# Loading the first channel weight of a mixer as full rows, in two halves of the contraction

## The chip, the cores and the metric

The kernel runs on one core of a Trainium2 chip. The metric is device time in microseconds (us) of one execution. The runs of one kernel are compared by their median; the profile is of one execution.

## What is computed

The input is a batch of 8, with 8 heads, 576 positions and a head size of 64. Attention is masked to a sliding window (heads 0 to 3: the last 32 positions; heads 4 to 7: every fourth of the last 128). Its output, 576 x 512 for each batch element, goes through a mixer over tokens and then one over channels:

```
x  = attention(q, k, v)                    # [8, 576, 512]
h  = relu(x^T @ w_tok1) @ w_tok2           # over the 576 tokens, 256 hidden
u  = x + h^T
h2 = relu(u @ w_ch1) @ w_ch2               # over the 512 channels, 1536 hidden
out = u + h2
```

The change concerns `w_ch1`, a 512 x 1536 matrix of float32 in memory, which the kernel holds as float16 on the chip for all eight batch elements.

## The kernel before

All matrix work is in float16 with float32 sums. Of the batch elements one (`b`) is in its channel mixer on TensorE, while the next ones are in their scores, their values and their token mixer. The order is written by hand: `gen_main(b)` yields the channel mixer piece by piece, and `interleave` puts the other steps between its pieces, by due times that are constants in the last loop of the kernel. Each engine works through its own list in that order and waits at an instruction whose input is not there; what stands behind it on the same engine waits too.

The channel mixer of one batch element is twelve blocks of 128 hidden channels (`mb`). For each block, TensorE sums four matmuls into a bank `gp`, one for each 128 of the 512 channels (`cb`), with a 128 x 128 piece of `w_ch1` as the weights. `w3_block(cb, mb)` names that piece. For batch element 0 the order of `cb` is 0, 1, 2, 3. Then twelve more matmuls for each output block sum into `yp`, with `w_ch2`. In rows of the profile and in rows of the order, the tiles of all weights are called `w`, so that `w_0`, `w_1` and `w_2` stand for `w3_0`, `w3_1` and `w3_2`.

`w3` is three tiles of 128 x 4 x 512. Tile `i` holds the columns 512 i to 512 i + 511 of all four `cb`, and so the blocks `mb` = 4 i to 4 i + 3. `load_w3(i)` loads one; the transfer reads 512 runs of 512 float32 and writes them as float16 (512 KB written). It is issued from GpSimd's queue (POOL), since it changes the type; the loads of q, k and v go through SyncE's queue (SP). Both queues are served by the same 16 DMA engines.

What surrounds the loads on POOL, in the start-up of the kernel: `cast_vd(0, 0)` and `cast_vd(0, 2)` cast the two halves of v of the dilated heads of batch element 0 to float16, from `l_vd`; `cast_vx` casts the last piece, from `l_vx`, for which TensorE waits in `values`. Then two copies make `w2p`, and `gate` writes one element of the tile `lt` of batch element 1. The first load of batch element 1 on SP overwrites that tile, so that all loads of batch element 1 start after it. The casts of batch element 1 (`casts1`: tails `c_t`, then q and k by turns into `c_q` and `c_k`) follow on POOL, and TensorE transposes their results (`tp_q`, `tp_k`, line 309).

Of the kernel before, what the change touches and what calls it, by code (L numbers as in the profile page):

```python
# [22 lines left out]
DCH = 1536  # L23
# [45 lines left out]
def kernel(  # L69
# [11 lines left out]
    nc = tc.nc  # L81
# [4 lines left out]
    def fixed(name, shape, dtype=FP16):  # L86
        return sb.tile(shape, dtype, tag=name, bufs=1, name=name)
# [3 lines left out]
    def bank(tag, bufs, name, dtype=FP32):  # L91

        if tag in turn:
            turn[tag] += 1
            tag, bufs = f"{tag}{turn[tag] % bufs}", 1
        return ps.tile([128, 512 if dtype == FP32 else 1024], dtype, tag=tag, bufs=bufs, name=name)

    def copy(eng, out, in_):
        if eng is nc.scalar:
            nc.scalar.copy(out=out, in_=in_)  # L100
        else:
            eng.tensor_copy(out=out, in_=in_)  # L102

    def relu(eng, out, in_):
        if eng is nc.scalar:
            nc.scalar.activation(out=out, in_=in_, func=AF.Relu)  # L106
        else:
            eng.tensor_scalar_max(out=out, in0=in_, scalar1=0.0)  # L108
# [39 lines left out]
    w2a = fixed("w2", [128, 2, 640])  # L148
    w2 = [w2a[:, i] for i in range(2)]
    w2p = [fixed(f"w2p_{i}", [128, 4, 128]) for i in range(2)]  # L150
    w3 = [fixed(f"w3_{i}", [128, 4, 512]) for i in range(3)]
    w4a = fixed("w4", [128, NMB, DM])
    w4 = [w4a[:, i] for i in range(NMB)]
    idle = fixed("idle", [128, 512])
# [109 lines left out]
    def cast_vn(b, s, eng):  # L264
        copy(eng, vv[b % 2][:, s, 0:4, 0:64], l32[(b, "vn")][:, s])

    def cast_vd(b, h, eng):
        copy(eng, vv[b % 2][:, 0:4, 4 + h:6 + h, 0:64],
             l32[(b, "vd")][:, h:h + 2].rearrange("m h r d -> m r h d"))
# [22 lines left out]
    def u16(b, s):  # L292
        if b not in u16w:
            u16w[b] = sb.tile([128, 4, 4, 128], FP16, tag="u16", bufs=2, name=f"u16_{b}")
        return u16w[b][:, :, s]

    def blocks4(ap):
        return ap.rearrange("p (x c) -> p x c", c=128)
# [448 lines left out]
    def gen_main(b):  # L747
        odd = b % 2
        order = CBS if b else range(4)
        m0 = 640 * odd  # L750

        def w3_block(cb, mb):
            return w3[mb // 4][:, cb, mb % 4:512:4]

        def gp_tails(g):
            p = bank("main", 3, f"gt_{b}_{g}")
            for i in range(4):
                for cb in order:
                    nc.tensor.matmul(  # L759
                        out=p[:, 128 * i:128 * i + 128], lhsT=w3_block(cb, 4 * g + i), rhs=uT[(b, cb)][1],  # L760
                        start=(cb == order[0]), stop=(cb == order[-1]))
            relu(nc.scalar, gta[:, 4 * g:4 * g + 4, 512:640],
                 p.rearrange("p (i t) -> p i t", t=128))

        for mb in range(NMB):
            p = bank("main", 3, f"gp_{b}_{mb}")
            for i, cb in enumerate(order):
                nc.tensor.matmul(out=p, lhsT=w3_block(cb, mb), rhs=uT[(b, cb)][0], start=(i == 0), stop=(i == 3))  # L768
                if i == 1:
                    yield 0.43  # L770
            relu(nc.vector if (mb % 2 == 1 if b == 0 else mb % 4 != 3 if b == 1 else mb in (1, 5)) else nc.scalar, gta[:, mb, m0:m0 + 512], p)
            yield 0.43
            if odd and mb in (3, 6, 9):
                gp_tails(mb // 3 - 1)
                yield 0.9
        last = b == B - 1
        for s in ((4, 0, 1, 2, 3) if odd else (0, 1, 2, 3)):
            p = bank("main", 3, f"yp_{b}_{s}")
            o32 = sb.tile([128, DM], FP32, tag="o32", bufs=4, name=f"o32_{b}_{s}")
            if s < 4:  # L780
                for half in range(2):
                    c = slice(256 * half, 256 * half + 256)
                    if last and s == 3 and half:
                        p = bank("main", 3, f"yq_{b}_{s}")
                    for mb in range(NMB):
                        a0 = m0 + (s if half else 128 * s)
                        nc.tensor.matmul(  # L787
                            out=p[:, c],
                            lhsT=gta[:, mb, a0:m0 + 512:4] if half else
                            gta[:, mb, a0:a0 + 128],  # L790
                            rhs=w4[mb][:, c], start=(mb == 0), stop=(mb == NMB - 1))
                        if mb == 5:
                            yield 0.65
                    if last and s == 3:
                        nc.vector.tensor_tensor(out=blocks4(o32[:, c]), in0=blocks4(p[:, c]), in1=u16(b, s)[:, 2 * half:2 * half + 2], op=ALU.add)
                    elif half:
                        nc.vector.tensor_tensor(out=blocks4(o32), in0=blocks4(p), in1=u16(b, s), op=ALU.add)  # L797
                    if half or (last and s == 3):
                        for i in ((half,) if last and s == 3 else (0, 1)):
                            d = slice(256 * i, 256 * i + 256)  # L800
                            o = out[b, 0:512, d].rearrange("(m r) c -> r m c", r=4)[s] if i else \
                                out[b, 128 * s:128 * s + 128, d]
                            nc.sync.dma_start(out=o, in_=o32[:, d])
                    yield 0.65
            else:
                for mb in range(NMB):
                    nc.tensor.matmul(out=p, lhsT=gta[:, mb, 512:640], rhs=w4[mb],  # L807
                                     start=(mb == 0), stop=(mb == NMB - 1))
                    if mb in (3, 7):
                        yield 0.87  # L810
                nc.vector.tensor_tensor(out=blocks4(o32), in0=blocks4(p), in1=u16t[b // 2], op=ALU.add)
                nc.sync.dma_start(out=out[b - 1, 512:S, :], in_=o32[0:64])
                nc.sync.dma_start(out=out[b, 512:S, :], in_=o32[64:128])
                yield 0.87
# [41 lines left out]
        nc.gpsimd.tensor_copy(out=t, in_=src)  # L856

    def load_w3(i):
        c = slice(512 * i, 512 * i + 512)
        nc.gpsimd.dma_start(out=w3[i], in_=moe_w_ch1[:, c].rearrange("(x p) c -> p x c", p=128))  # L860

    cast_qk(0, "q", 0, nc.scalar)
    cast_qk(0, "k", 0, nc.vector)
# [11 lines left out]
    for s in range(4):  # L875
        cast_vn(0, s, nc.gpsimd)
    nc.gpsimd.dma_start(out=w2a[:, :, 0:S], in_=moe_w_tok2.rearrange("(p j) t -> p j t", j=2))
    load_w3(0)
    cast_vd(0, 0, nc.gpsimd)
    cast_vd(0, 2, nc.gpsimd)  # L880
    load_w3(1)
    cast_vx(0, nc.gpsimd)
    nc.gpsimd.dma_start(out=w1t[1][64:128], in_=moe_w_tok1[512:S, :])
    for jb in range(2):
        nc.gpsimd.tensor_copy(
            out=w2p[jb], in_=w2[jb][:, 0:512].rearrange("p (m r) -> p r m", r=4))
# [94 lines left out]
    casts1 = cast_steps(1)  # L981
    for i in (0, 1):
        casts1[i]()
    load_w3(2)
    for i in (2, 3, 4, 5, 7, 6, 8, 9, 10, 11):
        casts1[i]()
    for i in range(3):
        nc.gpsimd.dma_start(
            out=w4a[:, 4 * i:4 * i + 4],
            in_=moe_w_ch2[512 * i:512 * i + 512, :].rearrange("(p i) c -> p i c", i=4))  # L990
# [82 lines left out]
```

## Time and profile before

| | |
|---|---|
| median of 3 runs | 288.79 us (288.76 to 289.51) |
| profiled execution, its own time | 289.66 us |
| span of the profile, first to last instruction | 287.8 us |
| TensorE (PE) busy | 276.8 us, 96% of the span |
| GpSimd (POOL) busy | 163.0 us, 57% |
| VectorE (DVE), ScalarE (ACT) busy | 132.1 us, 134.0 us |
| granted TensorE clock | 1.0 |

The profiled execution took 1.86 us more than its span, and 0.87 us more than the median of the runs. Times within the profile count from the start of the span. A share of DMA is the time that packets took, as a part of 16 engines' time; packets of one engine overlap, so that it can be over 100%. A DMA's megabytes are those written: for the weights, half of what is read.

### The profile page before, as it was taken

To read this page: it belongs to the slowest core of one execution; us is meant where nothing else is said; L and a number is where in the kernel's file an instruction comes from. 1 tells how busy PE (TensorE), PEld (TensorE's weight loads), DVE (VectorE), ACT (ScalarE), POOL (GpSimd) and SP (SyncE) were. 2 spreads that over 40 slices of the span, in tenths; PEclk is the share of its full clock that TensorE was granted. 3 is DMA by queue.
4 is the path that set the end of the run, shared out by engine and by line. 5 is a ranking of instruction groups with operands and counts; after the bars stand their busy time and mean duration, and the time that the engine had idled before them with its cause. 6 is when DMAs were issued, how large, how long until landed. Compare 5 with 4: busy or idle time off the path is not lost.

```text
span 287.8 us, 6995 instructions
## 1 busy us (share of the span) xinstructions
PE 276.8 (96%) x2838; PEld 210.9 (73%) x2838; DVE 132.1 (46%) x278; ACT 134.0 (47%) x265; POOL 163.0 (57%) x221
## 2 busy tenths in 40 slices
PE   5879999999999999999999999999999999999995
PEld 2777676888766886698776976797766966886594
DVE  7747658446764236414640164416440274421022
ACT  2854673263543804574447615482546534225500
POOL 6961860478865799449970999279952930000000
PEclk9999999999999999999999999999999999999999
DMA  7999999993999998979888978299974210431023
GB/s 218 263 211 218 283 225 207 320 218 82 328 210 192 264 264 230 139 164 350 226 159 182 330 224 186 57 219 329 193 150 95 85 64 2 91 112 37 0 76 108
DMA packets 105551, 52.63 MB, mean 183 GB/s; under 512 B 73872, under 2 KB 104464, under 8 KB 105520
## 3 DMA queue, kind: packets, MB, share of 16 engines
q1 hardware_dynamic: 101280, 47.07, 67.0%
q0 software_dynamic: 2640, 3.94, 8.0%
q10 hardware_dynamic: 1600, 1.18, 1.4%
q8 instruction: 22, 0.36, 0.6%
q14 instruction: 9, 0.07, 0.1%
HBM read 37.07 MB, written 9.44 MB: 162 GB/s over the span
## 4 chain that ended last, share of the span: by engine, by line
PE 80%; DMA 8%; DVE 3%; POOL 3%; issue 2%; ACT 2%; ACTq 1%; SPq 0%; POOLq 0%; DVEq 0%
PE yp L787 29%; PE gp L768 24%; DMA l_vd<-in_v_dram 4%; PE h1p L627 4%; PE yp L807 3%; DMA l_k<-in_k_dram 3%; PE up L639 3%; PE sc L510 3%; PE gt L759 3%; DVE xn L112 1%; DMA kr<-c_k 1%; PE h1p L625 1%; PE av L608 1%; PE up L650 1%; PE av L603 1%
## 5 line engine op out<-in xcount | busy, mean ns | idle before, releaser
L787 PE MATMUL yp<-w,gt 128*128 128x256 f16 x756 | 87.1, 273 | 0.0
L787 PEld LDWEIGHTS <-gt 128*128 128x128 f16 x768 | 78.6, 106 | 6.5
L106 ACT ACTIVATE gt<-gp 128x512 f16<-128x512 f32 x69 | 41.2, 597 | 76.3 <-PE gp L768 76.0
L768 PE MATMUL gp<-utd,w 128*128 128x512 f16 x144 | 54.7, 380 | 0.0
L768 PE MATMUL gp<-utm,w 128*128 128x512 f16 x144 | 54.6, 379 | 0.0
L768 PEld LDWEIGHTS <-w 128*128 128x128 f16 x384 | 39.2, 114 | 20.3 <-issue 0.5
L797 DVE TENSOR_TENSOR o<-yp,u 128x512 f32<-128x512 f32 x31 | 21.4, 691 | 63.1 <-PE yp L787 58.5
L112 POOL TENSOR_TENSOR attp<-attp,const 128x1280 f16<-128x1280 f16 x12 | 31.4, 2616 | 27.5 <-ACT attp L534 27.4
L112 DVE TENSOR_TENSOR xn<-av,rec 128x320 f16<-128x320 f32 x64 | 31.4, 491 | 2.2
L112 POOL TENSOR_TENSOR attd<-attd,const 128x1024 f16<-128x1024 f16 x12 | 25.3, 2132 | 1.6 <-ACT attd L534 1.6
L768 PE MATMUL gp<-uT,w 128*128 128x512 f16 x96 | 25.8, 379 | 0.0
L108 DVE TENSOR_SCALAR gt<-gp 128x512 f16<-128x512 f32 x27 | 18.5, 686 | 13.6 <-PE gp L768 13.1
L645 DVE TENSOR_TENSOR u<-up,xn 128x512 f16<-128x512 f32 x26 | 17.9, 690 | 7.5 <-PE up L639 7.5
L534 ACT ACTIVATE attp<-sc 128x480 f16<-128x480 f32 (+1 forms) x36 | 16.1, 536 | 7.4 <-PE sc L510 7.4
L102 POOL CAST c_k<-l_k 128x512 f16<-128x512 f32 x29 | 18.0, 628 | 1.9 <-DMA l_k<-in_k_dram 1.7
L102 POOL CAST c_q<-l_q 128x512 f16<-128x512 f32 x27 | 16.8, 629 | 3.1 <-DMA l_q<-in_q_dram 3.1
L616 DVE RECIPROCAL rec<-av 128x5 f32<-128x5 f32 x64 | 12.2, 190 | 13.8 <-PE av L613 13.7
L106 ACT ACTIVATE h<-h1p 128x256 f16<-128x256 f32 x29 | 11.1, 384 | 14.5 <-PE h1p L627 14.1
L399 POOL COPY kt<-kr 128x512 f16<-128x512 f16 x10 | 10.7, 1075 | 9.0 <-DMA kr<-c_k 9.0
L697 ACT COPY utd<-utm 128x512 f16<-128x512 f16 x12 | 12.8, 1135 | 4.1 <-DMA utm<-u 4.1
L102 POOL CAST vv<-l_vn 128x256 f16<-128x256 f32 x32 | 12.0, 420 | 4.3 <-DMA l_vn<-in_v_dram 4.1
L112 POOL TENSOR_TENSOR attt<-attt,const 128x512 f16<-128x512 f16 x12 | 14.0, 1165 | 0.0
(147 smaller groups left out, 459.9 us busy)
## 6 DMA issues: line engine op xcount, KB each, us to landing
out_dram<-o SPq DMA_DIRECT2D x72, 128.0 KB, 3.1
l_q<-in_q_dram SPq DMA_DIRECT2D x15, 512.0 KB, 7.2
l_k<-in_k_dram SPq DMA_DIRECT2D x14, 512.0 KB, 7.1
l_vn<-in_v_dram SPq DMA_DIRECT2D x32, 128.0 KB, 6.6
l_vd<-in_v_dram SPq DMA_DIRECT2D x16, 256.0 KB, 4.6
w<-in_moe_w_ch_dram POOLq DMA_DIRECT2D x6, 512.0 KB, 7.6
lt<-in_q_dram SPq DMA_DIRECT2D x8, 128.0 KB, 4.6
l_vt<-in_v_dram SPq DMA_DIRECT2D x8, 128.0 KB, 4.9
```

Of the source, the lines that this page charges most:

```text
L102: eng.tensor_copy(out=out, in_=in_)
L106: nc.scalar.activation(out=out, in_=in_, func=AF.Relu)
L108: eng.tensor_scalar_max(out=out, in0=in_, scalar1=0.0)
L112: eng.tensor_tensor(out=out, in0=x, in1=y, op=ALU.mult)
L534: nc.scalar.activation(out=out, in_=in_, func=AF.Exp, scale=0.125)
L616: nc.vector.reciprocal(out=rec[:, :, 0], in_=av[:, :, 64])
L627: nc.tensor.matmul(out=p, lhsT=w[:, s, j], rhs=x[:, s, c], start=False, stop=(s == 3))
L645: nc.vector.tensor_tensor(out=u16(b, s), in0=blocks4(p), in1=blocks4(xn[b][:, s]), op=ALU.add)
L697: nc.scalar.copy(out=natural(uTd[:, cb - 2]), in_=uTm[i][:, cb].rearrange("p r m -> p m r"))
L768: nc.tensor.matmul(out=p, lhsT=w3_block(cb, mb), rhs=uT[(b, cb)][0], start=(i == 0), stop=(i == 3))
L787: nc.tensor.matmul(out=p[:, c], lhsT=gta[:, mb, a0:m0 + 512:4] if half else gta[:, mb, a0:a0 + 128], rhs=w4[mb][:, c], start=(mb == 0), st ...
L797: nc.vector.tensor_tensor(out=blocks4(o32), in0=blocks4(p), in1=u16(b, s), op=ALU.add)
```

## The change

`w3` becomes two tiles of 128 x 2 x 1536. Tile `i` holds all 1536 columns of the `cb` 2 i and 2 i + 1. `load_w3(i)` reads 256 whole rows of 1536 float32 (768 KB written as float16). `w3_block` finds the same 128 x 128 piece in the new place, with the same stride of 4 elements. The first load is issued behind the first cast of `v` (`cast_vd(0, 0)`) and no longer ahead of it; the second keeps its place; the third, which stood among the casts of batch element 1, is gone.

```diff
-    w3 = [fixed(f"w3_{i}", [128, 4, 512]) for i in range(3)]
+    w3 = [fixed(f"w3_{i}", [128, 2, DCH]) for i in range(2)]
...
         def w3_block(cb, mb):
-            return w3[mb // 4][:, cb, mb % 4:512:4]
+            c0 = 512 * (mb // 4)
+            return w3[cb // 2][:, cb % 2, c0 + mb % 4:c0 + 512:4]
...
     def load_w3(i):
-        c = slice(512 * i, 512 * i + 512)
-        nc.gpsimd.dma_start(out=w3[i], in_=moe_w_ch1[:, c].rearrange("(x p) c -> p x c", p=128))
+        nc.gpsimd.dma_start(
+            out=w3[i], in_=moe_w_ch1[256 * i:256 * i + 256, :].rearrange("(x p) c -> p x c", p=128))
...
     nc.gpsimd.dma_start(out=w2a[:, :, 0:S], in_=moe_w_tok2.rearrange("(p j) t -> p j t", j=2))
+    cast_vd(0, 0, nc.gpsimd)
     load_w3(0)
-    cast_vd(0, 0, nc.gpsimd)
     cast_vd(0, 2, nc.gpsimd)
     load_w3(1)
     cast_vx(0, nc.gpsimd)
...
     for i in (0, 1):
         casts1[i]()
-    load_w3(2)
     for i in (2, 3, 4, 5, 7, 6, 8, 9, 10, 11):
         casts1[i]()
```

On POOL, in the start-up, the rows from the load of the token weight (`w_81`) to the cast of `l_vx` stood so before (the numbers behind the names differ by one between the two kernels and mean nothing):

```order
L877 DMA w_81<-in_moe_w_tok_dram 128x2x576
L860 DMA w_0_84<-in_moe_w_ch_dram 128x4x512
L102 CAST vv_69<-l_vd_123 128x4x2x64 [waits DMAHW5_49]
L102 CAST vv_69<-l_vd_123 128x4x2x64 [waits DMAHW6_49]
L860 DMA w_1_85<-in_moe_w_ch_dram 128x4x512
L102 CAST vt_71<-l_vx_124 128x4x64 [waits DMAHW7_49]
```

and so they stand now:

```order
L878 DMA w_81<-in_moe_w_tok_dram 128x2x576
L102 CAST vv_69<-l_vd_122 128x4x2x64 [waits DMAHW5_49]
L860 DMA w_0_84<-in_moe_w_ch_dram 128x2x1536
L102 CAST vv_69<-l_vd_122 128x4x2x64 [waits DMAHW6_49]
L860 DMA w_1_85<-in_moe_w_ch_dram 128x2x1536
L102 CAST vt_71<-l_vx_123 128x4x64 [waits DMAHW7_49]
```

The first load has moved behind a cast that waits for a transfer of v, and each load is half as large again.

On TensorE, the first matmuls of the channel mixer of batch element 0 (`gp_0` and the first of `gp_1`) stood so before:

```order
L768 LDWEIGHTS w_0_84 [waits DMASW4_49]
L768 MATMUL gp_0_659<-uT_0_549,w_0_84 128x512 [waits PE_49]
L768 LDWEIGHTS w_0_84
L768 MATMUL gp_0_659<-uT_1_565,w_0_84 128x512 [waits DVE_49]
L768 LDWEIGHTS w_0_84
L768 MATMUL gp_0_659<-uT_2_572,w_0_84 128x512 [waits Activation_49]
L768 LDWEIGHTS w_0_84
L768 MATMUL gp_0_659<-uT_3_579,w_0_84 128x512 [waits DVE_49]
```

and so they stand now:

```order
L769 LDWEIGHTS w_0_84 [waits DMASW4_49]
L769 MATMUL gp_0_657<-uT_0_548,w_0_84 128x512 [waits PE_49]
L769 LDWEIGHTS w_0_84
L769 MATMUL gp_0_657<-uT_1_564,w_0_84 128x512 [waits DVE_49]
L769 LDWEIGHTS w_1_85 [waits DMASW5_49]
L769 MATMUL gp_0_657<-uT_2_571,w_1_85 128x512 [waits Activation_49]
L769 LDWEIGHTS w_1_85
L769 MATMUL gp_0_657<-uT_3_578,w_1_85 128x512 [waits DVE_49]
```

The wait for the second transfer (`DMASW5`) now stands at the third matmul of the first block; before it stood at the first matmul of the fifth block (`gp_4`), 14 matmuls later. The number of instructions on TensorE is the same.

On POOL, the first casts of batch element 1 stood so before:

```order
L102 CAST c_t_609<-lt_589 128x512 [waits DMAHW0_49,DMAHW1_49,PE_49,Pool_49]
L102 CAST c_q_611<-l_q_0_585 128x512 [waits DMAHW2_49,PE_49,Activation_49]
L860 DMA w_2_86<-in_moe_w_ch_dram 128x4x512
L102 CAST c_k_614<-l_k_0_587 128x512 [waits DMAHW3_49,DVE_49,PE_49]
L102 CAST c_q_611<-l_q_0_585 128x512
```

and so they stand now:

```order
L102 CAST c_t_608<-lt_588 128x512 [waits DMAHW0_49,DMAHW1_49,PE_49,Pool_49]
L102 CAST c_q_610<-l_q_0_584 128x512 [waits DMAHW2_49,PE_49,Activation_49]
L102 CAST c_k_612<-l_k_0_586 128x512 [waits DMAHW3_49,DVE_49,PE_49]
L102 CAST c_q_610<-l_q_0_584 128x512
L102 CAST c_k_612<-l_k_0_586 128x512
```

The third load no longer stands between the first cast of q and the first of k.

## The prediction

> **What bounds the kernel now.** The page comes first, then TensorE's waits over the whole span, and its waits after the start-up alone.
>
> ```profile
> PE 276.8 (96%) x2838; PEld 210.9 (73%) x2838; DVE 132.1 (46%) x278; ACT 134.0 (47%) x265; POOL 163.0 (57%) x221
> PE av L611 <- POOL vt L102: 1.2, 1, 1.2
> ...
> PE h1p L625 <- DVE xn L112: 0.4, 1, 0.4
> PE sc L510 <- POOL kt L399: 0.2, 1, 0.2
> PE sm L423 <- ACT attd L488: 0.2, 1, 0.2
> PE av L608 <- DVE xn L112: 0.2, 1, 0.2
> ```
>
> TensorE is the bound, and its work stays the same. Of its waits, the 1.2 us on `vt` lies just behind the place where the loads move; the last four rows are all that it waits after 29 us, 1.0 us together. So the change can win at most about 1.2 us in the start-up, and everything that it makes late in the first 35 us is paid nearly in full. I therefore read the chain and POOL's timeline up to there.
>
> ```profile
> 11.76 7.27 DMA l_vd<-in_v_dram
> 19.08 0.63 POOL vv L102
> 19.71 0.68 POOL w L860
> 20.39 0.42 POOL vt L102
> 20.85 0.19 PE av L611
> ...
> 15.31 0.77 POOL L860 DMA_DIRECT2D w<-in_moe_w_ch_dram  x1
> 16.55 0.62 POOL L102 CAST vv<-l_vd 128x512 f16<-128x512 f32 x1 [0.46 <-DMA l_vd<-in_v_dram]
> ...
> 30.21 0.61 POOL L102 CAST c_q<-l_q 128x512 f16<-128x512 f32 x1 [0.80 <-DMA l_q<-in_q_dram]
> 30.76 0.77 POOL L860 DMA_DIRECT2D w<-in_moe_w_ch_dram  x1
> 31.67 0.61 POOL L102 CAST c_k<-l_k 128x512 f16<-128x512 f32 x1
> 32.22 0.62 POOL L102 CAST c_q<-l_q 128x512 f16<-128x512 f32 x1
> ...
> 31.79 0.39 PE L309 MATMUL tp_q<-const,c_q 128*128 128x128 f16 x4
> 32.93 0.39 PE L309 MATMUL tp_k<-const,c_k 128*128 128x128 f16 x4
> 33.15 0.39 PE L309 MATMUL tp_q<-const,c_q 128*128 128x128 f16 x4
> ```
>
> The first five rows are the chain: the second half of `l_vd` lands, then come cast, issue of the second weight load, cast of `l_vx`, and TensorE goes on. The rows from 30.21 show how little room batch element 1 has: its casts end 0.3 to 1.0 us before the transposes that read them (30.82 for 31.79, 32.28 for 32.93, 32.84 for 33.15).
>
> **The price of the new rows.** The weights' queue (q0) had the DMA engines almost to itself in two stretches, 18 to 20 us (`w_ch1`, runs of 1 KB written) and 42 to 44 us (`w_ch2`, runs of 4 KB):
>
> ```profile
> q0 software_dynamic: 373, 0.38, 118.1%
> ...
> q0 software_dynamic: 111, 0.41, 103.3%
> ```
>
> That is 0.19 MB in a us with short runs and 0.205 with long ones. The new runs (3 KB written) lie between; I take 0.20. All of `w_ch1` is 1.57 MB, 7.9 us. By the Trainium skill, page "DMA: Bandwidth & Descriptors", section Specifications, a run of 512 B is enough for full rate, so that longer runs should save nothing. By that the sum would take 0.19, 8.3 us; these rows disagree by 8%, and that is all that the new shape brings.
>
> **The first load, behind the first cast of v.** It is issued at 16.55 + 0.62 = 17.17 us and no longer at 15.31. POOL then waits for `l_vd` anyhow (until 19.08), so the issue costs nothing there. Does the second half of `l_vd` land earlier, with the weights out of its way? Queues at 16 to 18 us, then SP's queue at 18 to 20:
>
> ```profile
> q0 software_dynamic: 248, 0.25, 87.6%
> q1 hardware_dynamic: 452, 0.14, 28.7%
> ...
> q1 hardware_dynamic: 32, 0.01, 3.2%
> ```
>
> By 18 us v's data had gone through but for 0.01 MB. The token weight (0.29 MB) is ahead of `w_ch1` in q0 and accounts for most of the 0.25 MB. So the weights were hardly in v's way: I take 0, between 0 and -1.2 (the whole wait on `vt`).
>
> **When the second tile is there.** Issue to first packets I read from the gap in q0 when its ring ran dry, with the second load issued at 19.65 (20.9 to 21.9 us):
>
> ```profile
> q0 software_dynamic: 80, 0.07, 75.2%
> ...
> w<-in_moe_w_ch_dram POOLq DMA_DIRECT2D x1, 512.0 KB, 6.9
> ```
>
> 0.07 MB in that us, against 0.19: the load was only starting some 2 us after its issue. Then the first load starts at 17.2 + 2.0 = 19.2, the second follows without a gap, and both are through at 19.2 + 7.9 = 27.1, if nothing else runs. From 24 us SP's loads do. The second load of before took 6.9 us, of which 0.52 / 0.19 = 2.8 are transfer and 2.0 the start; the other 2.1 are sharing, stragglers and the last write. I add 1.0 to 2.1 of that: 28.1 to 29.2, centre 28.7. TensorE reads it at the third matmul of `gp`:
>
> ```profile
> 29.09 2.87 PE gp L768 x12
> ```
>
> So it is just in time: 0, and up to +1.0 if a us more goes to SP's packets.
>
> **The loads of batch element 1.** This is the term that decides. They share the engines, and there is little room (24 to 28 us, and 24 to 33.2):
>
> ```profile
> q1 hardware_dynamic: 1551, 0.76, 76.9%
> q0 software_dynamic: 237, 0.18, 29.6%
> ...
> q1 hardware_dynamic: 3621, 2.45, 93.8%
> q0 software_dynamic: 237, 0.18, 12.9%
> ```
>
> Before, 0.18 MB of weights were left when SP's packets began at 24 us. Now (24.0 - 19.2) x 0.20 = 0.96 MB are through by then, and 0.61 of 1.57 left: 0.43 MB more, 2.2 us of all engines. The third load, which used to follow from 33.2 us on, gives that back too late for the first casts. What could absorb it is slack in the engines: 24 to 33.2 us ran at 106.7%, and a stretch where both queues were full at 123.6%:
>
> ```profile
> q1 hardware_dynamic: 2179, 0.65, 63.6%
> q0 software_dynamic: 528, 0.52, 60.0%
> ```
>
> If the first stretch could be packed as the second, 14% of the 6 us until `l_k` lands, 0.8 us, come back. So the loads are late by 1.4 to 2.2 us; with half a us for the start of the first load, 0.9 to 2.7. I take 1.8.
>
> By the Trainium skill, "DMA: Bandwidth & Descriptors", Queues, rings and completion order, an engine serves its rings in turn, a packet at a time. That speaks against this change: a turn of the weights is now 3 KB, and SP's turn the same as ever. By it the weights finish earlier and SP's loads take the full 2.2 us, a time 0.4 us above mine. The last two rows (528 packets against 2179 in the same stretch) show no turn for turn of single runs, so I leave it a bound.
>
> What the lateness costs TensorE goes by landing and cast:
>
> ```profile
> l_q<-in_q_dram SPq DMA_DIRECT2D x1, 512.0 KB, 5.9
> l_k<-in_k_dram SPq DMA_DIRECT2D x1, 512.0 KB, 6.7
> ...
> 24.16 0.57 SPq L190 DMA_DIRECT2D l_q<-in_q_dram  x1
> 24.82 0.45 SPq L190 DMA_DIRECT2D l_k<-in_k_dram  x1
> ```
>
> `l_q` landed at 30.06 and `l_k` at 31.52. The cast of `l_k` can start 0.05 later, and the next cast of q ends 1.17 after that start (31.67 to 32.84): 32.74, plus the lateness d. The transpose at 33.15 needs it some 0.05 us earlier, so TensorE waits d - 0.36. The other two wait less (d - 0.97 at 31.79, d - 0.75 at 32.93), and these waits and that for the second tile overlap, so only the largest counts: 1.8 - 0.36 = +1.4.
>
> **The third load gone.** POOL saves its 0.77 us at 30.76, but that issue ended at 31.53 and `l_k` landed at 31.52: 0. From 33.2 on the loads of v get the engines back; TensorE waited for none of them, so 0, at best the 0.2 us on `kt`. `w3_block` keeps its stride and shape: 0.
>
> **Sum.** 0 + 1.4 + 0. Of the 1.0 us that TensorE waits after 29 us, I let 0.3 be swallowed (the waits on DVE and POOL, in so far as these do not move along): +1.1 us. On the profiled execution that is 289.66 + 1.1 = 290.8; it ran 0.87 us above the median, so I forecast 288.79 + 1.1 = 289.9 us.
>
> **Rivals.**
> - No change that can be measured (0.3% is 0.87 us, about what this kernel's runs can tell). The engines pack the extra bytes and d stays at 1.2 or less: a wait of 0.8, less 0.3, at most +0.5: 288.5 to 289.6. For it speak the 123.6%; against it, that SP's loads already had 93.8% to themselves.
> - Faster: the weights' descriptors and first packets did hold up the last bytes of `l_vd`. Each us by which it lands before 19.03 is a us for the cast of `l_vx` and for the gate of batch element 1; at 17.9 the wait on `vt` is gone, 288.79 - 1.2 = 287.6, if d is also under 0.4. It decides only if both hold; the 0.01 MB speak against it.
> - The second tile is late, at 31 us: TensorE stands at the third matmul for 1.9 us, less 0.3, with the transposes behind it on time: 290.4. For it speaks the longest of the weights' landings, that of a load queued behind two others; 19.65 + 10.6 is 30.3, and these loads are half as large again:
>
> ```profile
> DMA to landing us min/median/max: 5.5/7.4/10.6
> ```
>
> **How the numbers follow.** My forecast, the loads of batch element 1 late, has 0.42, with a range of its own of 289.3 to 291.1. The late tile has 0.12, no change 0.33, faster 0.13. Nearly all of the first two is over +0.87, but for 0.05 of the forecast's low end: slower 0.49, same 0.38, faster 0.13. The range goes from 288.2, into the no-change case and leaving out most of faster, to 291.2, with d = 2.7 (2.7 - 0.36 = 2.3, nothing swallowed, and 0.1 for the tile).
>
> **What would show it.** In the profile after: the first weight load issued near 17.2 us; the wait on `vt` still about 1.2 us; the second load landing near 28.7; `l_q` and `l_k` landing near 31.9 and 33.3; new waits of TensorE's `tp_q` or `tp_k` on POOL's `c_q` or `c_k`, 1 to 2 us together; and no wait above half a us at the third `gp`. I am wrong if `l_k` still lands before 32.7, if the wait on `vt` shrinks by over half, or if later stretches swallow more than the 1.0 us that they show.

## The result, and the profile after

The changed kernel takes 290.97 us (median of 6 runs, 289.94 to 292.02) against 288.77 us for the kernel before in the same comparison: a ratio of 1.0083, 95% interval 1.0061 to 1.0105, so 2.4 us slower (1.8 to 3.0). The forecast was 289.9, slower.

The first profile after is of the quickest of these six executions (289.94 us, span 288.1), so it shows the least that the change costs. Two more profiles of the changed kernel (292.43 and 291.36 us by themselves) lie above the median. First the page of the first profile, with the weights' queue, then its timeline of POOL:

```profile
PE 276.7 (96%) x2838; PEld 210.6 (73%) x2838; DVE 132.1 (46%) x278; ACT 133.9 (46%) x265; POOL 162.7 (56%) x220
q0 software_dynamic: 1600, 3.94, 7.3%
```

```profile
16.07 0.61 POOL L102 CAST vv<-l_vd 128x512 f16<-128x512 f32 x1 [0.88 <-DMA l_vd<-in_v_dram]
16.63 0.70 POOL L860 DMA_DIRECT2D w<-in_moe_w_ch_dram  x1
17.32 0.63 POOL L102 CAST vv<-l_vd 128x512 f16<-128x512 f32 x1
17.89 0.71 POOL L860 DMA_DIRECT2D w<-in_moe_w_ch_dram  x1
...
31.11 0.61 POOL L102 CAST c_q<-l_q 128x512 f16<-128x512 f32 x1 [0.69 <-DMA l_q<-in_q_dram]
32.62 0.61 POOL L102 CAST c_k<-l_k 128x512 f16<-128x512 f32 x1 [0.90 <-DMA l_k<-in_k_dram]
33.17 0.62 POOL L102 CAST c_q<-l_q 128x512 f16<-128x512 f32 x1
```

TensorE's work is the same (276.7 us). On POOL the first casts of q and of k of batch element 1 now both stand and wait for their loads (0.69 and 0.90 us); in the first profile of before, the cast of k had no such wait. The chain of the same profile runs through the load of k, issued at 23.58 and landed 8.89 us later, at 32.47:

```profile
23.58 8.89 DMA l_k<-in_k_dram
...
32.62 0.61 POOL c_k L102
33.23 0.57 POOL c_q L102
...
33.84 0.40 PE tp_q L309 x4
```

TensorE's waits from 28 to 36 us in this profile, then from 27 to 37 us in the third profile of the changed kernel:

```profile
PE tp_q L309 <- POOL c_q L102: 1.0, 2, 0.8
PE tp_k L309 <- POOL c_k L102: 0.2, 1, 0.2
PE gp L769 <- DMA w<-in_moe_w_ch_dram: 0.2, 1, 0.2
```

```profile
PE gp L769 <- DMA w<-in_moe_w_ch_dram: 1.6, 1, 1.6
PE tp_q L309 <- POOL c_q L102: 1.1, 2, 0.9
PE tp_k L309 <- POOL c_k L102: 0.2, 1, 0.2
```

So both of the waits that the prediction named are there: for the casts of batch element 1, 1.2 to 1.3 us, and for the second weight tile, 0.2 to 1.6 us. Both come from the same place: the DMA engines have more weights to move before 33 us. Here are both queues from 24 to 28 us, in the first profile after and then in a second profile of before:

```profile
q0 software_dynamic: 257, 0.53, 69.8%
q1 hardware_dynamic: 1083, 0.34, 42.3%
```

```profile
q1 hardware_dynamic: 1579, 0.89, 99.1%
q0 software_dynamic: 95, 0.07, 11.6%
```

In these four us 0.53 MB of weights (q0) now run beside the loads of batch element 1 (q1), for 0.07 MB then, and the loads get through 0.34 MB instead of 0.89.

**Where the two profiles mislead.** The spans differ by only 0.3 us (287.8 and 288.1), though the medians differ by 2.2. The first profile of before was itself a late execution. Here are the casts of v and the first channel matmuls in a second profile of before (288.46 us, span 286.6):

```profile
16.07 1.21 POOL L102 CAST vv<-l_vd 128x512 f16<-128x512 f32 x2
17.94 0.43 POOL L102 CAST vt<-l_vx 128x256 f16<-128x256 f32 x1
...
26.86 3.48 PE L768 MATMUL gp<-uT,w 128*128 128x512 f16 x14
...
32.09 0.40 PE L309 MATMUL tp_q<-const,c_q 128*128 128x128 f16 x4 [0.16 <-POOL c_q L102]
```

The second half of `l_vd`, at 19.03 us in the first profile, was there at once for the second cast. The first `gp` stands at 26.86 instead of 28.47 us, and the transpose that stood at 33.15 stands at 32.09. That transpose comes 1.06 us sooner, and the span is 1.2 us shorter. A third profile of before (288.93 us, span 287.1) has the second cast of v at 17.48 and the first `gp` at 27.93.

### The profile page after: what moved, and what is told of

Its sections match the earlier page's. It is cut to its first block, busy times and chain, and to the rows that moved or that the text cites. A ratio compares the mean times of both kernels' runs of the same rounds, so it can differ in the third digit from the quotient of the medians.

```text
span 288.1 us, 6994 instructions
## 1 busy us (share of the span) xinstructions
PE 276.7 (96%) x2838; PEld 210.6 (73%) x2838; DVE 132.1 (46%) x278; ACT 133.9 (46%) x265; POOL 162.7 (56%) x220
## 4 chain that ended last, share of the span: by engine, by line
PE 84%; DMA 8%; DVE 4%; ACT 1%; issue 1%; POOL 0%; ACTq 0%; POOLq 0%; DVEq 0%
PE yp L788 29%; PE gp L769 26%; PE h1p L627 4%; PE up L639 4%; PE yp L808 4%; PE gt L760 3%; DMA l_k<-in_k_dram 3%; PE sc L510 3%; DMA lt<-in_k_dram 3%; DMA l_vt<-in_v_dram 2%; DVE xn L112 2%; PE h1p L625 1%; PE av L603 1%; PE av L608 1%; PE up L650 1%; PE av L601 1%
## 5 line engine op out<-in xcount | busy, mean ns | idle before, releaser
L102 POOL CAST c_q<-l_q 128x512 f16<-128x512 f32 x27 | 17.1, 640 | 2.2 <-DMA l_q<-in_q_dram 2.2
L812 DVE TENSOR_TENSOR o<-yp,u16t 128x512 f32<-128x512 f32 x4 | 2.8, 691 | 23.8 <-PE yp L808 23.8
```

## The experiments

In what follows, "the mark" is the start of the transpose of the second head pair's q of batch element 1 (at 33.15 us in the first profile of before), as the last of TensorE's waits in the start-up stands in front of it. Four theories were on trial. Theory A: the weights' bytes that are ahead of the loads of batch element 1 set when `l_k` lands and so the mark. B: the long rows hold SP's rows up. C: in the kernel before, the early weight load holds up `l_vd`. D, added later: the loads of batch element 1 only start too late.

| kernel | ratio to before, 95% | span of the profile | `l_k` issued, landed | mark | mark to the end |
|---|---|---|---|---|---|
| before, three profiles | 1 | 287.8, 286.6, 287.1 | landed 31.52, 30.71, 30.61 | 33.15, 32.09, 32.61 | 254.67, 254.52, 254.46 |
| changed, three profiles | 1.0083 (1.0061 to 1.0105) | 288.1, 290.6, 289.5 | landed 32.47, 34.85, 33.86 | 33.84, 36.22, 35.24 | 254.25, 254.37, 254.27 |
| move alone | 1.0029 (1.0008 to 1.0049) | 288.5 | 23.60, 32.37 | 33.75 | 254.74 |
| rows alone | 1.0075 (1.0055 to 1.0095) | 290.1 | 23.98, 34.26 | 35.64 | 254.48 |
| third load early | 1.0085 (1.0065 to 1.0106) | 288.2 | 23.71, 32.50 | 33.88 | 254.34 |
| second issue later | 1.0010 (0.9991 to 1.0029) | 286.4 | 23.91, 30.84 | 32.22 | 254.22 |
| gate earlier | 1.0105 (1.0084 to 1.0126) | 288.2 | 21.59, 32.56 | 33.93 | 254.27 |
| four tiles | 0.9977 (0.9965 to 0.9990) | 286.3 | 23.40, 30.26 | 31.94 | 254.39 |
| four tiles, second issue later | 0.9989 (0.9973 to 1.0006) | 286.0 | landed 29.08 | 31.19 | 254.82 |

The last column settles where the time goes: from the mark to the end all 13 profiles take 254.2 to 254.8 us, while the mark itself varies from 31.2 to 36.2. And in nine of the 13, all three of the changed kernel among them, the mark lies 1.37 or 1.38 us behind the landing of `l_k`; in the other four (1.6 to 2.1 us) TensorE did not wait for these casts. The result is made ahead of the mark.

Each profile is of one execution, so the marks of two rows are not those of two medians. The profiled execution took 290.33 us for a median of 289.23 with the move alone, and 291.95 for 290.28 with the rows alone; 290.06 for 290.56 with the third load early, and 290.05 for 291.24 with the gate earlier. The first profile of the changed kernel is the quickest of its six as well.

**The move alone** (`e1_move`): three column tiles, but the first load behind the first cast of v.

```diff
-    load_w3(0)
     cast_vd(0, 0, nc.gpsimd)
+    load_w3(0)
```

> Three column tiles as before; only the first weight load moves behind the first cast of v. Theory A (the weights' bytes ahead of the loads of batch element 1 cost the time): the same 1.05 MB of weights is ahead of those loads and starts some 1 us later without the gap at 21 us, so it is through at about 25 to 25.5 us as before; time within 0.4 us of before. Theory B (the long rows take SP's turns on the DMA engines): no long rows, so also as before. Theory C (the move frees the second half of l_vd, which landed at 16.9 us in the changed kernel's profile and at 19.0 before): the wait of TensorE on vt, 1.2 us, goes away here, in every execution, and the time falls by 0.8 to 1.2 us.

Slower by 0.8 us (0.2 to 1.4), where A and B expected less than half a us either way and C a gain. C is out as a gain in time: nothing was won. A was off here too: the profile, which is of the slowest of eleven executions, lands the second weight load 10.1 us after its issue (27.98 us), and `l_k` at 32.37. From 24 to 28 us 0.20 MB of weights ran, for 0.18, 0.07 and 0.02 in the three profiles of before. So a later start of the weights, with the same bytes, seems to push a part of them into the loads of batch element 1. The direction fits A; the size I had not expected, and 0.02 MB more than in the first profile of before does not account for it.

**The rows alone** (`e2_rows`): the changed kernel with the first load ahead of the first cast of v again.

```diff
     cast_vd(0, 0, nc.gpsimd)
-    load_w3(0)
...
+    load_w3(0)
     cast_vd(0, 0, nc.gpsimd)
```

> Two full-row tiles as in the changed kernel, but the first load stays ahead of the first cast of v. Theory A: the weights start some 1.2 us earlier, so about 1.2 us less of them is left when the loads of batch element 1 begin; l_k lands about 1 us earlier than in the changed kernel, and of its 2.2 us over before 0.8 to 1.2 remain. Theory B: the long rows still take the turns, cost stays at 1.7 to 2.5 us over before. Theory C: the wait on vt is back, and the time is at least that of the changed kernel, 2 to 3.3 us over before.

2.2 us slower than before (1.6 to 2.7). The half of the loss that A expected back did not come: even the interval's lower end, 1.6, lies 0.4 above the 1.2 that A allowed. B's 1.7 to 2.5 was met, and so was C's 2 to 3.3; but the wait on `vt` that C expected is not in the profile. The two halves of the change, 0.8 and 2.2, do not add to the whole, 2.4; the intervals let that stand either way. Its profile lost time at the very start (TensorE waited 2.26 us for a cast, until 11.64, and the granted clock was 0.50 from 12.24 to 15.65 us), so its landings and marks are not compared with the others.

**The third load early** (`e3_third`): the column tiles with their short rows, all three loads ahead of the loads of batch element 1.

```diff
     cast_vx(0, nc.gpsimd)
+    load_w3(2)
...
         casts1[i]()
-    load_w3(2)
```

> Column tiles and their first two loads as before, but the third load is issued right behind the cast of l_vx, ahead of the loads of batch element 1. This is the change's bytes without its long rows and without the early need of the second half. Theory A: l_q and l_k of batch element 1 land 1.5 to 2.5 us later than before (31.6 to 32.6 and 33.0 to 34.0 us), TensorE waits for their casts, +1.2 to +2.2 us. Theory B: short rows share with SP's rows evenly, so l_q and l_k land at most 0.8 us later and the time is within 0.6 us of before. Theory C says nothing here.

This tells A from B. With no long row and no early need of a second half, the same bytes cost the same: 1.0085 against 1.0083. The waits are those of the first profile after:

```profile
31.81 0.40 PE L309 MATMUL tp_q<-const,c_q 128*128 128x128 f16 x4 [0.63 <-POOL c_q L102]
...
33.32 0.40 PE L309 MATMUL tp_k<-const,c_k 128*128 128x128 f16 x4 [0.19 <-POOL c_k L102]
33.88 0.40 PE L309 MATMUL tp_q<-const,c_q 128*128 128x128 f16 x4 [0.16 <-POOL c_q L102]
```

The row of the weights' queue from 20 to 24 us, when SP's queue moved nothing, first here (1 KB written in a run), then in the changed kernel (3 KB):

```profile
q0 software_dynamic: 823, 0.81, 123.6%
```

```profile
q0 software_dynamic: 288, 0.84, 106.5%
```

0.81 and 0.84 MB in 4 us: the full rows bring 4%. That is nearer to the Trainium skill ("DMA: Bandwidth & Descriptors", Specifications: 512 B is enough for full rate) than the 8% that I read from the rows of before.

**The second issue later** (`e4_issue`): before, with `load_w3(1)` behind `cast_vx`.

> Before, with the second weight load issued behind the cast of l_vx and no longer ahead of it. The issue took 0.68 us of the chain between the landing of l_vd and TensorE's wait on vt. Theory A: the weights begin 0.4 us later, with no more bytes, no cost; where the second half of l_vd lands late (19 us), TensorE's wait on vt shrinks from 1.2 to 0.5 us, so -0.3 to -0.7 us; where it lands early, 0. Theory C: the same.

No difference (-0.3 to +0.8 us). In its profile `l_vd` landed early (16.48), a case for which A expected 0, and TensorE waited 0.2 us each for the casts of k and of q, with the mark 1.38 us behind `l_k`. What the later issue gives when `l_vd` is late was not seen.

**The gate earlier** (`e7_gate`): the changed kernel, with the loads of batch element 1 let go some 2 us sooner.

```diff
-    gate(l32[(1, "t")][0:1, 0, 0:1], w2p[1][0:1, 0, 0:1])
+    gate(l32[(1, "t")][0:1, 0, 0:1], vt[0][0:1, 0, 0:1])
```

(with the loads of q and k of batch element 1, it stands right behind `cast_vx`.)

> The changed kernel, but the loads of batch element 1 are let go about 2 us earlier: the gate is written from the tile vt right behind the cast of l_vx, no longer from w2p. The same bytes in another order. Theory A (all these bytes must go through the 16 engines before both the second weight tile and l_k are there; before, 0.52 MB of them went later): l_k lands 0.5 to 1.5 us sooner than in the changed kernel, the second tile as much later (29 us and over), and TensorE's wait moves from the casts to the third matmul of gp; the time stays within 0.6 us of the changed kernel, so 1.6 to 2.8 us over before, more if the clock is cut during the wait. Theory D (only the late start of those loads costs): the time falls to within 0.8 us of before.

Still 3.0 us over before (2.4 to 3.6): D is out. `l_k` was issued 2 us sooner than in the changed kernel's first profile and landed at the same time, 32.56 for 32.47, while the wait at the second tile is 0.9 us against 0.2:

```profile
28.50 2.78 PE L769 MATMUL gp<-uT,w 128*128 128x512 f16 x12 [0.91 <-DMA w<-in_moe_w_ch_dram]
31.87 0.40 PE L309 MATMUL tp_q<-const,c_q 128*128 128x128 f16 x4 [0.58 <-POOL c_q L102]
```

The same bytes in another order only move the wait from one place to another. A's half a us sooner for `l_k` did not show.

**Four tiles** (`e5_quarters`): fewer bytes ahead, the opposite of the change. Column tiles of three blocks; `w_ch2` is loaded in four pieces of three blocks to match.

```diff
-    w3 = [fixed(f"w3_{i}", [128, 4, 512]) for i in range(3)]
+    w3 = [fixed(f"w3_{i}", [128, 4, 384]) for i in range(4)]
...
-            return w3[mb // 4][:, cb, mb % 4:512:4]
+            return w3[mb // 3][:, cb, mb % 3:384:3]
...
     load_w3(2)
+    load_w3(3)
```

> Column tiles of three blocks each (four loads of 384 columns, runs of 768 B written), the first two where the first two stood, the third and fourth where the third stood; w_ch2 in four loads to match, and the gate of batch element 2 on the second of them. So 0.79 MB of weights is ahead of the loads of batch element 1, against 1.05 before and 1.57 in the changed kernel. Theory A (bytes ahead of those loads set when l_k lands, and l_k sets the time): l_k lands 0.8 to 1.4 us sooner after the gate than before, TensorE's waits on c_q and c_k vanish, and the time falls by what these were before, 0.2 to 0.6 us; more only if the start-up before them was behind too. Theory B (the long rows cost the time): no change. If the third and fourth loads come late for blocks 6 and 9, it is slower.

This is faster than both kernels: 0.9977 (0.9965 to 0.9990), 0.7 us under before (A expected 0.2 to 0.6), and its slowest of 12 runs took 288.39 us, less than before's median in that comparison (288.54). The profile shows no wait of TensorE of over 0.15 us from 27 to 37 us:

```profile
27.25 3.48 PE L768 MATMUL gp<-uT,w 128*128 128x512 f16 x14
30.57 0.39 PE L309 MATMUL tp_q<-const,c_q 128*128 128x128 f16 x4
...
31.94 0.39 PE L309 MATMUL tp_q<-const,c_q 128*128 128x128 f16 x4
```

The bytes ahead of the loads of batch element 1 were 0.79, 1.05 and 1.57 MB in the four-tile kernel, in before and in the changed one; the times go with them, -0.7, 0 and +2.4 us. The gain is the smaller step; in this profile `l_k` is no longer what TensorE waits for. The move alone and the rows alone do not fit this order (the same bytes ahead as in before cost 0.8 us more, and an earlier start of the changed kernel's bytes gave nothing back), so the bytes are not the whole account. The four-tile kernel also changes the loads of `w_ch2` and which of them the gate of batch element 2 stands on; what these do by themselves was not tried, but from the mark to the end its profile takes 254.39 us, as the others do.

**Four tiles, second issue later** (`e6_quarters_issue`): both edits together.

> The four column tiles of three blocks, and the second load issued behind the cast of l_vx. Theory A: with l_k no longer last, TensorE's way through the start-up is the bound, and where l_vd lands late the 0.7 us of the issue come off the chain: 0.0 to 0.4 us less than with the four tiles alone, 0.6 to 1.1 us less than before. If the second tile (needed some 2.6 us behind the first gp) then comes late, TensorE waits at the fourth block and the gain is lost.

0.9989 (0.9973 to 1.0006): no gain over the four tiles alone, where A expected up to 0.4 us, and none over before that is clear of noise, where it expected 0.6 to 1.1. Its profile has the least span of all (286.0), but its runs scatter from 287.07 to 289.23 us.

**Before and after once more** (`b2`, `b3`, `a2`, `a3`): profiles only, shown above and below.

> The kernel before once more, for a second profile. Theory A: where the second half of l_vd lands at about 17 us, TensorE has no wait on vt, but waits 0.2 to 0.5 us for the casts of batch element 1; l_k lands near 31 us and the span is near 286.5. The first profile's late landing of l_vd (19.03) is then an accident of that execution. Theory C (the early weight load holds up l_vd): it lands at about 19 us here too.

> The kernel before, a third profile. Theory A: as for the second profile, l_vd at about 17 us or, by accident, 19; Theory C: 19 us in every profile of this kernel.

> The changed kernel once more, for a second profile. Theory A: waits of TensorE on c_q and c_k of 1 us or more, l_k landing some 11 us after the gate (before: some 9), and everything behind the transpose of c_q as long as in the other profiles, within 0.5 us.

> The changed kernel, a third profile, to see which of the two kinds of wait its executions have: at the casts of batch element 1 (the first profile, 1.4 us together) or at the second weight tile with a cut clock behind it (the second profile, 2.0 us). Theory A: one of these two, and 254.2 to 254.8 us from the transpose of the second head pair's q to the end.

In before, `l_vd` landed at 16.59 and 17.43 us, with the weight load in front of the cast as ever, so the late 19.03 is no rule of this order: C is out here too. The second profile of before waits only 0.16 us for a cast, less than expected, and the third nothing. The second profile of the changed kernel has none of the 1 us or more that A expected at the casts; it waits 2.0 us for the second tile instead. The third waits at both places.

## Why the prediction was right, and where it was not

**The cause held.** The loads of batch element 1 land late behind 0.5 MB more of weights, and TensorE waits for their casts. I forecast 0.61 MB of weights left at 24 us: from 24 to 28 us 0.53, 0.70 and 0.53 MB ran in the three profiles of the changed kernel. I forecast `l_k` at 33.3 us; they have 32.47, 34.85 and 33.86. I forecast the second tile at 28.7; it landed at 28.10, 30.40 and 29.43. The first load was issued at 16.5 to 17.1 us, for 17.2. In all three the mark lies 1.37 or 1.38 us behind `l_k`.

**Where it failed by its own signs.** I had written that I would be wrong if `l_k` landed before 32.7 us or if the wait on `vt` shrank by over half. The first happened in the quickest execution (32.47). The second happened in all three profiles; but in the second and third profile of before there is no wait on `vt` either, so this was a sign of one execution and not of the change. Nor did the third `gp` keep to half a us: the late tile, which I gave 0.12, made it wait 1.6 and 2.0 us in two of three profiles. It did not set the mark there, as the part on the clock shows.

**The size was half.** I forecast a loss of 1.1 us, and 2.2 (the two medians) to 2.4 (the ratio) was measured. That 290.97 lies inside the range, whose upper end of 291.2 I had reached with loads 2.7 us late, is owed to the width of the range and not to the sum.

**The step that was mis-sized most is the base.** The mark at 33.15 in the first profile of before gave me 290.8 us for the profiled execution, close to the 290.97 measured; then I took 0.87 us off, as that execution was so much over the median. But these 0.87 us were not a surcharge on any kernel: they go with the late `l_vd` of that execution, as the other two profiles show, with `l_vd` at 16.59 and 17.43 and the mark 1.06 and 0.54 us earlier. In the profiles of the changed kernel `l_k` sets the mark, so nothing of them comes off. (In all three `l_vd` landed by 17.4 us; what a late one would add there was not seen.) The 1.1 us would have been 1.1 + 0.87 = 2.0. The slack of 0.36 us ahead of the transpose was of that one execution too: the second profile of before has none, the third 0.6 us.

**The lateness was too small as well.** I took the loads 1.8 us late. `l_k` landed 0.95, 3.33 and 2.34 us behind the 31.52 of the first profile of before, and later still against the other two (30.71 and 30.61). A part of the 1.8 rested on slack in the engines, which was to give back 0.4 of 2.2 us and did not show. I had read it from the share of DMA, and that is the time of packets and not what they move: in the rows above, a stretch at 123.6% moved 0.81 MB, and one as long at 106.5% moved 0.84 MB.

**What held of the rest.** The move of the first load gave nothing back, as taken; but alone it costs 0.8 us, where I had 0. "Swallowed 0.3" held against the first profile of before: from the mark to the end 254.67 there, 254.25 to 254.37 after; against the other two it is 0.1 to 0.3. The price of a byte was near: 0.20 MB in a us taken, 0.21 measured.

**A cut clock, which I had not seen coming.** In the second profile after, TensorE waited 2.04 us for the second tile. First the timeline around the twelve matmuls behind the wait, there and in the third profile; then the second profile by stretches (the column behind the engines is the granted clock):

```profile
30.45 4.47 PE L769 MATMUL gp<-uT,w 128*128 128x512 f16 x12 [2.04 <-DMA w<-in_moe_w_ch_dram]
```

```profile
29.47 2.78 PE L769 MATMUL gp<-uT,w 128*128 128x512 f16 x12 [1.63 <-DMA w<-in_moe_w_ch_dram]
```

```profile
30.00:31.00 1.00, 0.55 (x2) 0.26 (x3) 0.00 (x0) 0.00 (x0) 0.00 (x0) 0.88 1.14 307
31.00:32.00 1.00, 1.00 (x4) 0.41 (x3) 0.00 (x0) 0.60 (x1) 0.00 (x0) 0.50 1.08 330
32.00:33.00 1.00, 1.00 (x4) 0.35 (x3) 0.01 (x1) 0.00 (x0) 0.61 (x1) 0.50 1.10 352
33.00:34.00 1.00, 1.00 (x3) 0.30 (x2) 0.68 (x1) 0.00 (x0) 0.51 (x1) 0.50 1.11 352
34.00:35.00 1.00, 1.00 (x9) 0.61 (x8) 0.00 (x0) 0.48 (x1) 0.10 (x2) 0.91 1.08 338
```

The same twelve matmuls took 1.7 us more, at a granted clock of 0.50. The wait of 2.0 us and the cut held TensorE for 3.7 us, but they did not make this execution longer than `l_k` did. POOL's casts and the end of TensorE's wait in the second profile:

```profile
34.99 0.61 POOL L102 CAST c_k<-l_k 128x512 f16<-128x512 f32 x1 [0.90 <-DMA l_k<-in_k_dram]
35.55 0.62 POOL L102 CAST c_q<-l_q 128x512 f16<-128x512 f32 x1
...
35.90 0.39 PE L309 MATMUL tp_k<-const,c_k 128*128 128x128 f16 x4
36.22 0.40 PE L309 MATMUL tp_q<-const,c_q 128*128 128x128 f16 x4
```

The cast of k began 0.14 us behind the landing of `l_k` (34.85), the cast of q behind it ended at 36.17, and the mark, 36.22, lies 1.37 us behind the landing, as in the profiles without a cut. Where it need not wait, the transpose of q starts 0.22 us after that of k (32.93 and 33.15 in the first profile of before); here it is 0.32, so TensorE still waited some 0.1 us for the cast. The wait for the tile and the cut filled time in which TensorE would have waited for the casts anyway. In the third profile it waited for the casts outright, behind 1.6 us for the tile.

The Trainium skill, "TensorE: Matmul & The Clock Gate", Part 1, says that the clock is halved after an idle window of about 3.4 us. Here less idle time was enough. The start-ups of the 13 profiles show two cuts, each 3.41 us long: this one, from 30.77 us, and the one in the profile of the rows alone, from 12.24 us. Each began a whole number of 3.41 us (7 and 2) after the first entry in that trace's record of the clock (6.87 and 5.41 us). If stretches of 3.41 us are laid from that entry, these are the ones ahead of the two cuts, and, last, the one in the third profile that holds most of its wait of 1.6 us:

```profile
27.35:30.77 3.42, 1.33 (x11) 0.69 (x11) 1.03 (x2) 0.65 (x2) 0.00 (x0) 1.00 1.15 247
```

```profile
8.83:12.24 3.41, 1.15 (x20) 0.98 (x18) 0.86 (x2) 1.86 (x4) 3.24 (x12) 1.00 1.21 291
```

```profile
27.95:31.36 3.41, 1.89 (x9) 1.06 (x10) 0.55 (x2) 0.60 (x1) 0.15 (x1) 1.00 1.11 303
```

TensorE was busy for 1.33 and 1.15 of 3.4 us ahead of the cuts, and for 1.89 us where none followed. That idle time is counted in such stretches is my reading of these three; no run was made to test it.

**What stays open.** Why the second half of `l_vd` landed 2 us late in the first profile of before was not tried. In that profile one 16 KB packet of instructions ran on an engine between 16 and 18 us; other profiles have such a packet too. The three profiles of the changed kernel leave nothing of the loss to the tile's wait, and the early third load, without such a wait, costs the same; the other executions were not profiled. Why the move alone cost 0.8 us, and why the earlier start in the rows alone gave nothing back, is not shown. Nor is it shown what parts two executions of the changed kernel: the first and the third profile moved the same 0.53 MB of weights from 24 to 28 us, and `l_k` landed 1.4 us apart.

## What to carry to other kernels

- Where transfers bound a start-up, count the bytes that are ahead of the first load that someone waits for. Larger pieces, fewer issues and longer rows do not help if they bring bytes forward that are needed later; smaller first pieces did (0.7 us here).
- Splitting a weight by the contraction makes the first matmul group need all of it; splitting by columns lets the work start with the first piece. (Here the wait that came of it, up to 2.0 us, was hidden by the wait for the casts.)
- A wait that is seen need not be one that is paid. Ask what else would have held the engine at that place: here the mark followed `l_k`, with and without the tile's wait.
- One profile is one execution. Before slack is read from it, ask whether it stands for the median. If the new bound is another one, the profile's distance to the median is not to be taken off.

## What the runs showed of the hardware

- Runs of 1 KB and 3 KB written went through the engines at 0.20 and 0.21 MB in a us: the length of the rows hardly mattered. The share of DMA went the other way (123.6% and 106.5%), so a share over 100% is no measure of what is moved.
- Waits of TensorE of 2.0 and 2.3 us (the second and the rows-alone profile) were each followed by 3.41 us at half the clock; a wait of 1.6 us was not. Twelve matmuls of 128x512 took 4.47 us then, for 2.78.
